# Zero columns in a turned weight, paired slope stores, and one norm asked for earlier, in a four-layer forward and backward pass

## Chip, cores and metric

The kernel runs on one core of one Trainium2 chip. The metric is device time in microseconds of one execution. Each kernel is executed several times, and the median of the runs is compared. One execution is also recorded by the hardware profiler; the views that are quoted come from that record.

## The reference

The reference is four residual layers and the gradients of all their inputs. Layers 0 and 2 are linear attention (A), layers 1 and 3 a gated block (B). S = 2048, D = 512, F = 1376, 32 heads of 16, everything in bfloat16. A and B use the same weights both times.

```
x = x + A(layernorm(x))        # wqkv, wo: phi(q) (phi(k)^T v), normalised, @ wo
x = x + B(layernorm(x))        # h = sigmoid(x @ w_gate) * (x @ w_up);  h @ w_down
x = x + A(layernorm(x))
x = x + B(layernorm(x))
out, vjp = jax.vjp(f, A_x, A_wqkv, A_wo, B_w_gate, B_w_up, B_w_down)
return out, *vjp(grad_out)
```

## The kernel before

The 2048 rows are 16 tiles of 128 rows (`st`), in 4 blocks of 4 tiles (`NBLK`, `NB`; a block has `SB` = 512 rows). The F = 1376 columns are 11 chunks of 128 (`NFC`). 1376 is 10 x 128 + 96, so the last chunk overlaps the one before it: `FC0[10]` is 1248, and its first 32 columns (`FDUP`) are columns that chunk 9 holds too. Work on chunk 10 must not count these 32 twice.

The order of the work is written out by hand with Python generators: while layer l goes through its blocks, steps of the next layer are put between its chunks. Each engine runs its own list in order, and a tile framework adds the semaphores. TensorE (PE) has the matmuls, VectorE (DVE), ScalarE (ACT) and GpSimd (POOL) the elementwise work; SyncE (SP) issues most DMAs in one order, POOL some stores.

**Forward of layer 1** is `b_fwd`. For each block and chunk `glu` (L641 to L663) makes g and u (8 matmuls of 128 x 512), then on ACT the tanh (L655) and the slope's first half into `sd` (L656), on DVE `hh` (L657), and the second half of `sd` either on DVE (L659, `fused`, every odd chunk) or on ACT and POOL (L661, L662). `sd` tiles hold two chunks each and come from a pool of 7 slots, which attention's `pe_t` tiles share in part of the time. `store` (L677 to L679) writes `hh` and `sd` to DRAM when the next chunk is under way, on SP. At the start of the next block `down` (L682 to L690) multiplies `hh` with w_down: for each of 4 tiles chunks 0 to 9, and then chunk 10 for the 4 tiles.

**The norm ahead of a layer** is `LN.one`. For layer 1 it goes in pairs of tiles: the squares on ACT (L315), the reciprocal root on POOL (L317, L318), the norm on DVE (L320), the transposed copy `hT` by a DMA transpose on SP (L323). `AFwd.out` asks for the norm of a pair as soon as layer 0's output of that pair is added; a condition on L583 leaves out the last pair of a block in blocks 1, 2 and 3 of layer 0. Those pairs (tiles 6 and 7, 10 and 11, 14 and 15) are then asked for at chunk 10 of the block of layer 1 that goes before (`ln.need` in `b_fwd`).

**Layer 3** is `b_both`, forward and backward in one. It needs w_down turned (`wdT`, three DMA transposes by `turn_wd`, which cut w_down as `SETS` does: 512, 512 and 352 columns) and w_up and w_gate turned (`wuT`, `wgT`). The latter are loaded by `load_b_bwd` while block 0 goes through its chunks: for each one DMA transpose of chunks 0 to 9, one of chunk 10, and then a POOL memset that clears the first 32 rows of chunk 10. Per chunk `b_both` makes g, u and the gradient `dhh` (4 matmuls on `wdT`), on DVE `scale` multiplies `dhh` into `sd`, which is from then on the gradient `dd`. In blocks 1 to 3 `turn_dd` turns each chunk by a DMA transpose into `nat_t` tiles of 4 chunks, which `flush_nat` stores; block 0 stores its chunks unturned. At chunk 2 of block 1 (chunk 1 later) come `down` of the block before (4 x 11 matmuls, L728) and `dh_b` (L819 to L826), which goes through the 11 chunks of `wuT` and then the 11 of `wgT` for each tile.

**Later**, `wdT` comes back from DRAM (`wdT_d`) for layer 1's backward, `b_bwd`, which also loads the stored slopes (`sh_t`, 4 or 3 chunks a load). Everything after that is the weights' gradients.

Of the kernel before, what the change touches and what calls it, by code (L numbers as in the profile page):

```python
# [69 lines left out]
@with_exitstack  # L70
def kernel(
    ctx: ExitStack,
    tc: tile.TileContext,
    A_x: bass.AP,
    A_wqkv: bass.AP,
    A_wo: bass.AP,
    B_x: bass.AP,
    B_w_gate: bass.AP,
    B_w_up: bass.AP,
    B_w_down: bass.AP,  # L80
    grad_out: bass.AP,
    out_0: bass.AP,
    out_1: bass.AP,
    out_2: bass.AP,
    out_3: bass.AP,
    out_4: bass.AP,
    out_5: bass.AP,
    out_6: bass.AP,
):
    nc = tc.nc  # L90
    assert tuple(A_x.shape) == (1, S, D) and tuple(grad_out.shape) == (1, S, D)
    assert tuple(A_wqkv.shape) == (D, 3 * D) and tuple(A_wo.shape) == (D, D)
    assert tuple(B_w_gate.shape) == (D, F) and tuple(B_w_up.shape) == (D, F) and tuple(B_w_down.shape) == (F, D)
    k = K()
    k.nc, k.tc = nc, tc
    k.st = nc.gpsimd
    k.x_in = A_x.rearrange("b s d -> (b s) d")
    k.g_in = grad_out.rearrange("b s d -> (b s) d")
    k.out0 = out_0.rearrange("b s d -> (b s) d")
    k.out1 = out_1.rearrange("b s d -> (b s) d")  # L100
    k.outs = dict(wqkv=out_2, wo=out_3, wg=out_4, wu=out_5, wd=out_6)
    k.w_in = dict(wqkv=A_wqkv, wo=A_wo, wg=B_w_gate, wu=B_w_up, wd=B_w_down)

    pool = lambda name, bufs, **kw: ctx.enter_context(tc.tile_pool(name=name, bufs=bufs, **kw))
    consts, resid, k.keep = pool("consts", 1), pool("resid", 1), pool("keep", 1)

    k.small = pool("small", 6)
    k.p_h, k.p_hT = pool("h", 4), pool("hT", 4)
    dram = pool("dram", 1, space=DRAM)

    build_consts(k, consts)
    k.xs = [resid.tile([P, D], F32, name=f"x{st}") for st in range(NST)]
    k.sv = []
    for l in range(4):
        d = dict(h=dram.tile([S, D], BF16, name=f"sv_h{l}"))
        if l % 2 == 0:
            for nm in ("dqT", "dkT"):
                d[nm] = dram.tile([D, S], BF16, name=f"sv_{nm}{l}")
            for nm in ("hT", "pkT", "qr", "qn"):
                d[nm] = dram.tile([NBLK, P, (2 if nm == "qr" else 1) * NB * D], BF16, name=f"sv_{nm}{l}")  # L120
            d["E"] = dram.tile([D, D], BF16, name=f"sv_E{l}")
            d["M"] = dram.tile([D, D], BF16, name=f"sv_M{l}")
            d["kvT"] = dram.tile([NDC * P, P], BF16, name=f"sv_kvT{l}")
            d["CT"] = dram.tile([D, D], BF16, name=f"sv_CT{l}")
            d["dkvT"] = dram.tile([NDC * P, P], BF16, name=f"sv_dkvT{l}")
        else:
            d["hhT"] = dram.tile([F, S], BF16, name=f"sv_hhT{l}")
            d["ddT"] = dram.tile([2, F, S], BF16, name=f"sv_ddT{l}")
            if l == 3:
                d["g"] = k.g_in  # L130
                d["wd"] = dram.tile([F, D], F32, name="sv_wd3")
                d["ddN"] = dram.tile([NBLK, len(SETS), P, 2, NB, D], BF16, name="sv_ddN3")
            else:
                d["g"] = dram.tile([S, D], BF16, name=f"sv_g{l}")
                d["sd"] = dram.tile([NBLK, NFC, P, 2 * SB], BF16, name=f"sv_sd{l}")
        k.sv.append(d)
    k.rstd = [k.keep.tile([P, NST], F32, name=f"rstd{l}") for l in range(4)]
    k.A = {l: {} for l in (0, 2)}
    k.wT = [dram.tile([P, NDC * D], BF16, name=f"wT{i}") for i in range(6)]
    k.wdT_d = dram.tile([P, NDC * F], BF16, name="wdT_d")  # L140
    k.turned = []
    k.gns, k.gTs, k.nats = {}, {}, []

    k.wb = ExitStack()
    k.ps = pool("ps", 4, space=PSUM)
    forward(k)
    backward(k)


# [275 lines left out]

def turn_wd(k, t, i):
    c0, w = SETS[i]
    k.nc.sync.dma_start_transpose(out=t[:, :, c0:c0 + w], in_=k.w_in["wd"][c0:c0 + w, :])


def load_b_bwd(k, t, nm, first):
    nc = k.nc
    held(k, first, nc.sync.dma_start_transpose(out=t[:, 0:NFC - 1, :], in_=k.w_in[nm][:, 0:(NFC - 1) * P]))
    nc.sync.dma_start_transpose(out=t[:, NFC - 1, :], in_=k.w_in[nm][:, F - P:F])
    nc.gpsimd.memset(t[0:FDUP, NFC - 1, :], 0.0)


def add_x(k, st, y_ps, x=None):
# [8 lines left out]
class AFwd:  # L447
# [130 lines left out]
    def out(self, b, j):  # L578
        k, nxt = self.k, self.nxt
        y_ps = k.bank([P, D], F32, name="y_ps")  # L580
        mm4(k, y_ps[:], lambda c: self.pe[b, c // 2][:, 0, c % 2, rows(j)], lambda c: self.M[:, c, :])
        add_x(k, b * NB + j, y_ps, None if self.l else narrow(k, b * NB + j))
        if j % 2 and (b < 2 or self.l == 0) and not (b and j == NB - 1 and self.l == 0):  # L583
            nxt.need(b * NB + j)

    def second(self, nxt):
# [32 lines left out]
        for nm, t in (("E", E), ("M", M), ("kvT", kvT)):  # L619
            k.st.dma_start(out=sv[nm][:].rearrange("(c p) e -> p c e", p=P), in_=t[:])  # L620
        if l == 2:
            k.wdT = k.p_wa.tile([P, NDC, F], BF16, name="wdT", tag="wkvo")
            turn_wd(k, k.wdT, 0)
            last_grads(k, 0)
        for j in range(NB):
# [45 lines left out]
def b_fwd(k, l, ln, nxt):  # L671
    nc, sv = k.nc, k.sv[l]
    hhs, late = {}, []

    def store():

        b, fc, hh, sd = late.pop()  # L677
        store_hh(k, sv, b, fc, hh, nc.sync)
        nc.sync.dma_start(out=sv["sd"][b, fc], in_=sd.rearrange("p a b -> p (a b)"))  # L679

    def down(b):
        ys = [k.bank([P, D], F32, name="y_ps") for _ in range(NB)]  # L682
        for fcs in (range(NFC - 1), (NFC - 1,)):
            for j in range(NB):
                for fc in fcs:
                    nc.tensor.matmul(ys[j][:], lhsT=hhs[b][fc][:, rows(j)], rhs=k.wd[:, fc, :],
                                     start=(fc == 0), stop=(fc == NFC - 1))
        for j in range(NB):
            add_x(k, b * NB + j, ys[j])

    for b in range(NBLK):
        hhs[b] = []
        if b:
            down(b - 1)
        for fc in range(NFC):
            hh, sd = glu(k, ln.hT[b], fc, fc % 2 == 1, b == fc == 0)
            hhs[b].append(hh)
            if late:
                store()
            late.append((b, fc, hh, sd))  # L700
            if fc == NFC - 1:
                ln.need((b + 1) * NB + NB - 1)
            if b and fc in (2, 4):
                nxt.need((b - 1) * NB + (1 if fc == 2 else 3))
            yield b, fc
    store()
    down(NBLK - 1)
    nxt.need(NST - 1)
# [10 lines left out]
def b_both(k, l, ln, ctx):  # L719
# [17 lines left out]
    def scale(b, fc, dhh, dd):  # L737
        k.last_mul = nc.vector.tensor_tensor(dd, dhh[:].unsqueeze(1).to_broadcast([P, 2, SB]), dd, ALU.mult)  # L738
        if b:
            turn_dd(k, sv, b, fc, dd)  # L740
        else:
            store_dd(k, sv, b, fc, dd, nc.sync)

    late = []
    for b in range(NBLK):
# [4 lines left out]
        for fc in range(NFC):  # L750
            hh, dd = glu(k, ln.hT[b], fc, first=b == fc == 0)
            ps = k.bank([P, SB], F32, name="dhh_ps")
            mm4(k, ps[:], lambda c: k.wdT[:, c, FC0[fc]:FC0[fc] + P], lambda c: gTs[b][:, c, :])
            dhh = k.p_dhh.tile([P, SB], BF16, name="dhh_t")
            nc.scalar.mul(dhh[:], ps[:], 0.5)
            if late:
# [35 lines left out]
def turn_dd(k, sv, b, fc, dd):  # L792

    i, f = divmod(fc, 4)
    p0 = FDUP if fc == NFC - 1 else 0
    if f == 0:
        k.nat = k.p_nat.tile([P, 2, NB, D], BF16, name="nat_t")
    k.nc.sync.dma_start_transpose(
        out=k.nat[:, :, :, f * P - p0:(f + 1) * P - p0].rearrange("p a j f -> p (a j) f"),
        in_=dd.rearrange("p a s -> p (a s)"))  # L800
    if f == 1:
        flush_nat(k)
    if f == 3 or fc == NFC - 1:
        w = SETS[i][1]
        k.nats.append((sv["ddN"][b, i, :, :, :, 0:w], k.nat[:, :, :, 0:w]))

# [26 lines left out]
def backward(k):  # L833
    nc, tc = k.nc, k.tc
    with ExitStack() as ctx:
# [8 lines left out]
        k.woT = wab.tile([P, NDC, D], BF16, name="woT")  # L844
        k.wqkvT = wab.tile([P, 3 * NDC, D], BF16, name="wqkvT")
        sv, k.n_t, k.turn = k.sv, NB, True
        k.wdT = w_pool(k, "wdT").tile([P, NDC, F], BF16, name="wdT")
        k.fill = Fill(k)
        a_bwd(k, 2, False)
        b_bwd(k, 1)  # L850
# [48 lines left out]
def b_bwd(k, l):  # L899
    nc, sv = k.nc, k.sv[l]  # L900
    with ExitStack() as ctx:
# [23 lines left out]
        for b in range(NBLK):  # L925
            for f0, nf in FGRP:
                sh = k.p_sh.tile([P, 4, 2, SB], BF16, name="sh_t", tag="sh")
                nc.sync.dma_start(out=sh[:, 0:nf].rearrange("p f a s -> p f (a s)"),
                                  in_=sv["sd"][b, f0:f0 + nf].rearrange("f p s -> p f s"))
                for fc in range(f0, f0 + nf):  # L930
                    i = fc - f0
                    ps = k.bank([P, SB], F32, name="dhh_ps")
                    mm4(k, ps[:], lambda c: k.wdT[:, c, FC0[fc]:FC0[fc] + P], lambda c: gTs[b][:, :, c, :])
                    dhh = p_g.tile([P, SB], BF16, name="dhh_t")
                    nc.scalar.mul(dhh[:], ps[:], 0.5)  # L935
                    dd = p_dd.tile([P, 2, SB], BF16, name="dd_t")
# [363 lines left out]
```

## Time and profile before

| quantity | value |
|---|---|
| runs (us) | 1104.85, 1107.46, 1107.54, 1108.09, 1112.91 |
| median of the runs | 1107.54 |
| profiled execution, its own time | 1108.09 |
| its span, first to last instruction | 1106.1 |
| mean granted TensorE clock | 0.997 |
| PE, share of the span | 96% |
| DVE, ACT, POOL | 50%, 40%, 27% |
| mean DMA rate | 235 GB/s |

The span is what the record covers; the own time also has what lies around it (1.99 us). In lines of a timeline the first number is the start in us from the span's start, the second the time from the first to the last instruction of the group, then engine, line, operation, result and inputs, sizes, the number of instructions, and in brackets how long the engine stood idle before it and what released it. In the view of waits the three numbers are the total, the number of times and the longest. In the view of stretches the first numbers are the stretch and its length, then the busy time of PE, weight loads, DVE, ACT and POOL, and at the end the granted clock, the share of the DMA engines in use (it can pass 1) and GB/s.

### The profile page before, as it was taken

How to read it: one execution, taken by the hardware profiler on the slowest of the kernel's cores; microseconds unless marked ns; L12 is line 12 of the kernel's file. 1: busy time of each engine (PE TensorE's matmuls, PEld its weight loads, DVE VectorE, ACT ScalarE, POOL GpSimd, SP SyncE). 2: the span in 40 equal slices, each digit the busy share in tenths (PEclk: the TensorE clock that was granted, in tenths of full speed). 3: DMA queues.
4: the chain of work that ended last, by engine and by line, in shares of the span. 5: the costliest groups of instructions: out<-in, count | busy, mean ns of one | idle time of the engine just before them, and what ended most of it. 6: DMA issues, size and time to landing. Idle time of an engine off the chain costs nothing.

```text
span 1106.1 us, 15309 instructions
## 1 busy us (share of the span) xinstructions
PE 1065.0 (96%) x5448; PEld 494.7 (45%) x5448; DVE 552.9 (50%) x1029; ACT 445.4 (40%) x930; POOL 302.9 (27%) x404
## 2 busy tenths in 40 slices
PE   6989899999999999999999999999999999999998
PEld 3444343444434444444444444444444444465443
DVE  7686764669825445444767435556876200001110
ACT  4476775547744646453224434434235200000010
POOL 5333433203632616141532210002623100011120
PEclk9999999999999999999999999999999999999999
DMA  9987987689995979799997997868989899599990
GB/s 268 277 234 241 282 219 221 197 199 230 299 226 120 272 181 266 210 231 281 318 326 213 225 269 221 241 183 243 357 250 337 221 244 216 124 204 255 268 207 31
DMA packets 394972, 259.99 MB, mean 235 GB/s; under 512 B 305744, under 2 KB 356720, under 8 KB 393872
## 3 DMA queue, kind: packets, MB, share of 16 engines
q1 hardware_dynamic: 379648, 208.91, 75.4%
q0 software_dynamic: 15248, 50.11, 13.2%
q8 instruction: 42, 0.69, 0.3%
q14 instruction: 34, 0.28, 0.1%
HBM read 77.73 MB, written 106.76 MB: 167 GB/s over the span
## 4 chain that ended last, share of the span: by engine, by line
PE 53%; DMA 3%; issue 2%; ACT 2%; POOL 1%; DVE 1%; SPq 0%; ACTq 0%; DVEq 0%; POOLq 0%
PE dw_ps L1244 18%; PE dh_ps L916 7%; PE dhh_ps L196 4%; PE dh_ps L1089 4%; PE dh_ps L825 3%; PE dw_ps L1262 3%; PE dpk_ps L196 2%; PE dh_ps L1080 2%; PE CT_ps L1009 2%; PE y_ps L196 2%; PE fill_ps L252 1%; PE dq_ps L196 1%; PE g_ps L196 1%; PE u_ps L196 1%; DMA qp_l<-sv_qr 1%
## 5 line engine op out<-in xcount | busy, mean ns | idle before, releaser
L1244 PE MATMUL dw_ps<-set_t,rows_t 128*128 128x512 bf16 (+1 forms) x1024 | 204.4, 362 | 0.0
L1244 PEld LDWEIGHTS <-rows_t 128*128 128x128 bf16 x1024 | 100.1, 98 | 103.6
L662 POOL TENSOR_TENSOR sd_t<-sd_t,hh_t 128x512 bf16<-128x512 bf16 x68 | 81.4, 1197 | 156.2 <-DVE hh_t L657 104.6
L1169 DVE CAST dw_new<-dw_ps 128x512 bf16<-128x512 f32 (+1 forms) x20 | 12.4, 653 | 186.9 <-PE dw_ps L1244 160.9
L1169 ACT CAST dw_new<-dw_ps 128x512 bf16<-128x512 f32 (+1 forms) x20 | 10.5, 561 | 225.7 <-PE dw_ps L1244 188.1
L886 ACT ACTIVATE t_sb<-dh_ps,rstd 128x512 f32<-128x512 f32 x64 | 43.5, 680 | 129.3 <-PE dh_ps L825 90.0
L196 PE MATMUL g_ps<-hT_t,wg 128*128 128x512 bf16 (+1 forms) x360 | 91.6, 377 | 3.8 <-DMA hT_t<-h_t 2.5
L196 PE MATMUL dhh_ps<-gT_t,wdT 128*128 128x512 bf16 x352 | 90.5, 379 | 2.9 <-ACT dhh_t L935 2.9
L196 PE MATMUL u_ps<-hT_t,wu 128*128 128x512 bf16 (+1 forms) x360 | 91.6, 377 | 0.5 <-DVE hh_t L657 0.2
L916 PE MATMUL dh_ps<-wgT,dd_t 128*128 128x512 bf16 x176 | 66.7, 379 | 0.0
L916 PE MATMUL dh_ps<-wuT,dd_t 128*128 128x512 bf16 x176 | 66.7, 379 | 0.0
L657 DVE SCALAR_TENSOR_TENSOR hh_t<-sd_t,u_ps 128x512 bf16<-128x512 bf16 x88 | 59.5, 679 | 10.2 <-ACT sd_t L656 9.5
L738 DVE TENSOR_TENSOR sd_t<-dhh_t,sd_t 128x1024 bf16<-128x1024 bf16 x44 | 30.4, 690 | 63.0 <-POOL sd_t L662 61.6
L1170 POOL DMA_DIRECT2D out_dram<-dw_new x36 | 19.3, 541 | 155.5 <-DVE dw_new L1169 136.0
L656 ACT ACTIVATE sd_t<-g_ps,onef 128x512 bf16<-128x512 f32 x88 | 60.4, 690 | 2.6
L937 DVE TENSOR_TENSOR dd_t<-dhh_t,sh_t 128x1024 bf16<-128x1024 bf16 x44 | 29.9, 690 | 60.5 <-ACT dhh_t L935 55.0
L655 ACT ACTIVATE g_ps<-g_ps 128x512 f32<-128x512 f32 x88 | 52.5, 600 | 11.7 <-PE g_ps L196 11.3
L196 PEld LDWEIGHTS <-wg 128*128 128x128 bf16 x360 | 34.6, 98 | 45.4 <-issue 3.8
L196 PEld LDWEIGHTS <-wdT 128*128 128x128 bf16 x352 | 34.4, 98 | 44.6 <-issue 3.7
L196 PEld LDWEIGHTS <-wu 128*128 128x128 bf16 x360 | 35.4, 98 | 42.1 <-issue 1.8
L825 PEld LDWEIGHTS <-sd_t 128*128 128x128 bf16 x352 | 34.5, 98 | 41.5
L916 PEld LDWEIGHTS <-dd_t 128*128 128x128 bf16 x352 | 34.4, 98 | 41.6
(167 smaller groups left out, 1837.2 us busy)
## 6 DMA issues: line engine op xcount, KB each, us to landing
sv_sd<-sd_t SPq DMA_DIRECT2D x44, 256.0 KB, 3.3
sv_ddT<-dd_t SPq DMA_DIRECT2D x40, 256.0 KB, 4.8
sv_h<-h_t POOLq DMA_DIRECT2D x16, 512.0 KB, 5.1
sv_qr<-pe_t POOLq DMA_DIRECT2D x16, 512.0 KB, 5.1
sh_t<-sv_sd SPq DMA_DIRECT2D x8, 1024.0 KB, 6.6
rows_t<-sv_h SPq DMA_DIRECT2D x16, 512.0 KB, 6.8
sv_ddN<-nat_t SPq DMA_DIRECT2D x6, 1024.0 KB, 4.8
set_t<-sv_ddN SPq DMA_DIRECT2D x12, 512.0 KB, 6.6
```

The costliest lines, as they stand in the source:

```text
L196: i = k.nc.tensor.matmul(out, lhsT=lhs(c), rhs=rhs(c), start=(c == 0), stop=(c == n - 1))
L655: nc.scalar.activation(g_ps[:], g_ps[:], ACT.Tanh, scale=-0.5)
L656: nc.scalar.activation(sd[:, 0, :], g_ps[:], ACT.Identity, bias=k.onef[:], scale=-1.0)
L657: nc.vector.scalar_tensor_tensor(hh[:], sd[:, 0, :], 0.5, u_ps[:], ALU.mult, ALU.mult)
L662: nc.gpsimd.tensor_tensor(sd[:, 1, :], sd[:, 1, :], hh[:], ALU.mult)
L738: k.last_mul = nc.vector.tensor_tensor(dd, dhh[:].unsqueeze(1).to_broadcast([P, 2, SB]), dd, ALU.mult)
L825: k.nc.tensor.matmul(dh_ps[:], lhsT=dds[fc][:, a, rows(j)], rhs=(k.wuT, k.wgT)[a][:, fc, :], start=(i == 0), stop=(i == 2 * NFC - 1))
L886: nc.scalar.activation(t_sb[:], dh_ps, ACT.Identity, scale=rstd, accum_out=c1[:])
L916: nc.tensor.matmul(acc[b][j][:], lhsT=dd[:, a, rows(j)], rhs=(k.wuT, k.wgT)[a][:, fc, :], start=(fc == 0 and a == 0), stop=(fc == NFC - 1 ...
L1089: nc.tensor.matmul(dh[j][:], lhsT=lhs(j, c), rhs=rhs(c), start=False, stop=stop and c == NDC - 1)
L1244: k.nc.tensor.matmul(ps[ic][:, 0:w], lhsT=h_m[:, ic * P:(ic + 1) * P], rhs=t_m, start=(m == 0), stop=(m == n - 1))
L1262: k.nc.tensor.matmul(p[0:r, :], lhsT=t[:, f:f + r], rhs=g_t, start=(i == 0 and st == 0), stop=(i == len(srcs) - 1 and st == NST - 1))
```

## The change

Four edits, the first and the last of which belong together:

1. `wdT` gets 11 x 128 = 1408 columns instead of 1376. Chunk 10 is columns 1280 to 1407 of it, of which the first 32 are cleared by one POOL memset and the other 96 are w_down's last rows, turned by a DMA transpose of their own. `dhh` of chunk 10 is then zero in its first 32 rows, and `wuT` and `wgT` are no longer cleared there. `wdT_d` in DRAM grows with it.
2. The slopes of layer 1 are stored two chunks at a time, in a DRAM layout that has the partition first.
3. The condition on L583 now leaves out the last pair only where b is 1. The norms of tiles 10, 11 and of 14, 15 are asked for as soon as layer 0's output is added.
4. `turn_dd` turns chunk 9 after chunk 10: chunk 10's turned form has 32 columns of zeros that lie where chunk 9's last 32 columns go, and chunk 9 overwrites them.

```diff
-                d["sd"] = dram.tile([NBLK, NFC, P, 2 * SB], BF16, name=f"sv_sd{l}")
+                d["sd"] = dram.tile([P, NBLK * NFC, 2 * SB], BF16, name=f"sv_sd{l}")
...
-    k.wdT_d = dram.tile([P, NDC * F], BF16, name="wdT_d")
+    k.wdT_d = dram.tile([P, NDC * NFC * P], BF16, name="wdT_d")
...
 def turn_wd(k, t, i):
     c0, w = SETS[i]
+    n = (NFC - 1) * P
+    if i == len(SETS) - 1:
+        k.nc.gpsimd.memset(t[:, :, n:n + FDUP], 0.0)
+        k.nc.sync.dma_start_transpose(out=t[:, :, n + FDUP:], in_=k.w_in["wd"][n:F, :])
+        w = n - c0
     k.nc.sync.dma_start_transpose(out=t[:, :, c0:c0 + w], in_=k.w_in["wd"][c0:c0 + w, :])
...
     nc.sync.dma_start_transpose(out=t[:, NFC - 1, :], in_=k.w_in[nm][:, F - P:F])
-    nc.gpsimd.memset(t[0:FDUP, NFC - 1, :], 0.0)
...
-        if j % 2 and (b < 2 or self.l == 0) and not (b and j == NB - 1 and self.l == 0):
+        if j % 2 and (b < 2 or self.l == 0) and not (b == 1 and j == NB - 1 and self.l == 0):
             nxt.need(b * NB + j)
...
-        nc.sync.dma_start(out=sv["sd"][b, fc], in_=sd.rearrange("p a b -> p (a b)"))
+        n = b * NFC + fc
+        if n % 2:
+            nc.sync.dma_start(out=sv["sd"][:, n - 1:n + 1], in_=sd[:].rearrange("p n a s -> p n (a s)"))
...
         if b:
+            if fc == NFC - 2:
+                return
             turn_dd(k, sv, b, fc, dd)
+            if fc == NFC - 1:
+                turn_dd(k, sv, b, fc - 1, dds[b][fc - 1])
...
-            mm4(k, ps[:], lambda c: k.wdT[:, c, FC0[fc]:FC0[fc] + P], lambda c: gTs[b][:, c, :])
+            mm4(k, ps[:], lambda c: k.wdT[:, c, rows(fc)], lambda c: gTs[b][:, c, :])
...
-    if f == 3 or fc == NFC - 1:
+    if f == 3 or fc == NFC - 2:
...
-                                  in_=sv["sd"][b, f0:f0 + nf].rearrange("f p s -> p f s"))
+                                  in_=sv["sd"][:, b * NFC + f0:b * NFC + f0 + nf])
```

`dhh` in layer 1's backward uses `rows(fc)` of `wdT` in the same way.

More of the change, by code (lines that the diff above doesn't have):

```diff
@@ L621, in second @@
         if l == 2:
-            k.wdT = k.p_wa.tile([P, NDC, F], BF16, name="wdT", tag="wkvo")
+            k.wdT = k.p_wa.tile([P, NDC, NFC * P], BF16, name="wdT", tag="wkvo")
             turn_wd(k, k.wdT, 0)
@@ L699, in b_fwd @@
                 store()
-            late.append((b, fc, hh, sd))
+            late.append((b, fc, hh, k.sd2))
             if fc == NFC - 1:
@@ L846, in backward @@
         sv, k.n_t, k.turn = k.sv, NB, True
-        k.wdT = w_pool(k, "wdT").tile([P, NDC, F], BF16, name="wdT")
+        k.wdT = w_pool(k, "wdT").tile([P, NDC, NFC * P], BF16, name="wdT")
         k.fill = Fill(k)
@@ L932, in b_bwd @@
                     ps = k.bank([P, SB], F32, name="dhh_ps")
-                    mm4(k, ps[:], lambda c: k.wdT[:, c, FC0[fc]:FC0[fc] + P], lambda c: gTs[b][:, :, c, :])
+                    mm4(k, ps[:], lambda c: k.wdT[:, c, rows(fc)], lambda c: gTs[b][:, :, c, :])
                     dhh = p_g.tile([P, SB], BF16, name="dhh_t")
```

## The prediction

> **What bounds the kernel now.** I read the page's engine table first, then the waits of PE, then the timeline around its long waits, and last the granted clock in those stretches.
>
> ```profile
> PE 1065.0 (96%) x5448; PEld 494.7 (45%) x5448; DVE 552.9 (50%) x1029; ACT 445.4 (40%) x930; POOL 302.9 (27%) x404
> ```
>
> PE is busy for 1065.0 of 1106.1 us, so it is idle for 41.1 us. The change leaves the number and the order of PE's instructions alone. The time can therefore move only through PE's waits and through its clock. The next view lists what PE waited for, by total:
>
> ```profile
> PE y_ps L196 <- DVE hh_t L657: 2.7, 1, 2.7
> PE g_ps L196 <- DMA hT_t<-h_t: 2.5, 1, 2.5
> ...
> PE y_ps L686 <- DVE hh_t L657: 2.0, 1, 2.0
> ```
>
> These three single waits lie at edited code; the rest of the 41 us does not. PE's timeline places two of them:
>
> ```profile
> 167.22 9.66 PE L686 MATMUL y_ps<-wd,hh_t 128*128 128x512 bf16 x44
> 179.41 1.74 PE L196 MATMUL g_ps<-hT_t,wg 128*128 128x512 bf16 x4 [2.53 <-DMA hT_t<-h_t]
> ...
> 316.60 7.29 PE L196 MATMUL y_ps<-wd,hh_t 128*128 128x512 bf16 x33
> 326.58 4.10 PE L196 MATMUL y_ps<-wd,hh_t 128*128 128x512 bf16 x11 [2.70 <-DVE hh_t L657]
> 330.52 2.54 PE L825 MATMUL dh_ps<-wuT,sd_t 128*128 128x512 bf16 x11
> ```
>
> The first is block 3 of layer 1, waiting for the transposed norm of tiles 14 and 15. The second is the last output tile of block 0 in layer 3. It is put down to DVE, whose hh frees a PSUM bank, but DVE itself had stood 12.29 us behind a POOL product, and POOL's timeline shows why:
>
> ```profile
> 323.58 0.51 POOL L435 MEMSET wuT<- 32x512 bf16 x1 [11.03 <-DMA wuT<-in_B_w_up_dram]
> 324.06 1.14 POOL L662 TENSOR_TENSOR sd_t<-sd_t,hh_t 128x512 bf16<-128x512 bf16 x1
> ```
>
> A memset of 0.51 us waits for the load of wuT, and product, DVE and PE wait behind it. The last view gives stretches of PE, DVE, ACT and POOL with the granted clock third from the end:
>
> ```profile
> 179.60:183.00 3.40, 3.40 (x9) 1.18 (x8) 0.00 (x0) 1.82 (x5) 0.00 (x0) 0.50 0.00 1
> 326.30:329.80 3.50, 3.22 (x8) 1.13 (x8) 1.51 (x3) 0.32 (x1) 1.67 (x2) 0.51 1.08 245
> 135.20:138.60 3.40, 3.39 (x16) 1.57 (x17) 1.60 (x3) 0.08 (x1) 1.99 (x2) 1.00 1.01 353
> ```
>
> After each of the two long waits PE ran 3.4 us at half clock (8 or 9 matmuls instead of 16). After the 2.00 us wait at 135 it did not.
>
> **The sum is made against 1108.09 us**, the profiled execution (span 1106.1, and 1.99 around it), 0.55 above the median of the runs, 1107.54. A matmul of 512 columns takes 0.216 us (four in 0.86).
>
> **Norm no longer deferred (tiles 10, 11 and 14, 15 of layer 1).** Before, the norm of tiles 14 and 15 is asked for at chunk 10 of block 2: squares on ACT at 166.42 and 168.20, transpose issued on SP at 173.21, landed 6.2 later, 179.4. The rows of x were ready on DVE at 160.7. Now it is asked for right after them. Moved are one ln_neg, two squares (0.71 each), two POOL steps (0.19 and 0.71), two DVE norms (0.54) and the transpose on SP. On SP it now passes some seven stores (hhT and sd). I put its issue at 167 and its landing at 173 to 174, before 176.7, where PE asks. The wait of 2.53 goes, and with it the half clock behind it, 3.40 x 0.50 = 1.7. What is late next: the squares now stand ahead of chunk 9's tanh and slope on ACT. Its hh was done at 168.5 and is needed at 167.22 + 9 x 0.216 = 169.2. With two squares ahead I put it at 169.5, a new wait of 0.4 in the middle of down's matmuls, with all of PE's list behind it. Its ends are 0, the row where it was not late, and 2.0, the row of block 1; the value is nearest to zero because ACT only reorders work that it did anyway. In block 1 (tiles 10, 11) the same move puts POOL's rstd ahead of a product. The hh that ends the 2.00 us wait then comes 0.45 earlier: -0.45, with ends -0.5 and +1.1 (another product of 1.14 ahead of it). Sum of the part: -2.53 - 1.7 + 0.4 - 0.45 = -4.28.
>
> **No memsets of wuT and wgT.** POOL's product then runs when its inputs are there, near 313. The 2.70 wait goes, and its half clock, 3.50 x 0.49 = 1.7. What is late next: down(0) begins at 316.60 and takes 44 x 0.216 = 9.5, to 326.1; the 11 matmuls on wuT take 2.4, to 328.5. wuT's tail landed before 323.6, so nothing waits there. The first matmul on wgT then wants the body of that load:
>
> ```profile
> 321.42 5.59 SPq L433 DMA_TRANSPOSE wgT<-in_B_w_gate_dram  x1
> ...
> DMA to landing us min/median/max: 3.8/6.3/8.7
> ```
>
> It lands at 321.42 + 8.7 = 330.1; before, PE came there at 332.89 and waited for nothing. New wait 330.1 - 328.5 = 1.65, with all of PE's list behind it. Its ends are 0 (the load lands earlier, with SP less full) and 4.4 (the whole gain lost, because the stores that POOL held back now share the DMA engines, at a share of 1.08 already). I take 1.65, since nothing that the load itself waits for is edited. Sum: -2.70 - 1.7 + 1.65 = -2.75.
>
> **The zero columns.** One POOL memset of 128 x 128 elements is added: between 0.2 (Z_t, 128x128) and 0.51 (32x512). It waits for the matmuls that read wo (its slot held wo before) and stands ahead of the store of M, which waits for what those matmuls make; POOL idled 2.20 us there: nothing, and 0.5 for that store without the cover. The third turn of w_down (SP, 3.20 us at 264.17) becomes two transposes. The second costs SP some 1.25 (the row of wuT's tail), SP idles 267.4 to 269.6, and the columns are first used near 305: nothing. wdT goes to DRAM and back 2.3% larger (10 us a way); the load at 578.94 has 37 us before its first use: nothing. Chunk 9 turned after chunk 10 adds no instruction. It delays one store of a set and changes places on SP with one load of g. The next hf_t load still lands near 507.9 and is used at 513.45: a cover of 5.5 us.
>
> **Slopes stored in pairs.** 22 stores of 512 KB instead of 44 of 256 KB.
>
> ```profile
> L679 SPq DMA_DIRECT2D sv_sd<-sd_t x44: 319/520/1405, 78.6 to 205.4; - x44
> sv_sd<-sd_t SPq DMA_DIRECT2D x44, 256.0 KB, 3.3
> sv_hT<-hT_t SPq DMA_DIRECT2D x8, 512.0 KB, 4.3
> ```
>
> SP saves 22 x 0.52 = 11.4 us of issue between 77 and 205, where only the late transpose above waits on it; that is in the first part already. The landing of one pair is about 1 us later (4.3 against 3.3). A pair is stored when the next chunk is under way, 5.6 us after its slot was taken, so the slot is free near 10 us. While four of the seven slots hold pe_t (75 to 125 us, 19 chunks of 2.6 us), three slots cycle in 3 x 2 x 2.6 = 15.6. The cover is some 5.7 us: nothing. The loads of slopes in layer 1's backward move the same bytes: nothing.
>
> **Total:** -4.28 - 2.75 = -7.03, so 1108.09 - 7.0 = 1101.1.
>
> [...] The two half-clock terms rest on the rows 0.50 and 0.51. [...]
>
> **Rivals.** First, the next transfer takes the place of the memset: wgT lands later still, as the freed stores share its engines. For it: the share of DMA stands above 1.0 there. Against it: the load's own issue is untouched. Then layer 3 gains nothing, 1108.1 - 4.3 = 1103.8. Second, the half-clock stretches come back behind other waits (1.65 is not far from 2.53): 1108.1 - 3.6 = 1104.5; against it stands the 2.00 us wait with full clock after it. Third, on the other side, the pair holds its slot too long. It decides from a landing of 15.6 - 5.6 = 10 us; the longest of the 44 stores was 5.9. At 11.5 us each of some ten pairs up to 125 us holds ACT's next slope, and PE, for 1.5: +15 - 7 = +8, 1116. Fourth, the change does not do what it says: hT still lands behind the stores on SP, and other loads take the rest, near 1107.5.
>
> **How the numbers follow.** My forecast gets 0.55, the rivals 0.19, 0.09, 0.09 and 0.08. By 0.5% (5.5 us, about what a measurement of this kernel can tell from no change) faster means below 1102.0. The forecast's own range is 1099 (both new waits at zero) to 1103 (they double); about 0.44 of its 0.55 lies below 1102. The first rival gives 0.05 there, the second 0.01: faster 0.50. Slower, above 1113.1, is the third rival, 0.09. The rest, 0.11 + 0.14 + 0.08 + 0.08, is 0.41. The range runs from 1098.0 (the forecast's lower end, and a run 1 us below it; the five runs spread further) to 1107.5, the fourth rival's value, and leaves out the third.
>
> **What would show it.** Right: no PE wait for hT_t in layer 1; no memset at wuT or wgT; granted clock 1.00 in the stretches that answer to those at 0.50 and 0.51; a wait of about 1.6 us for wgT ahead of dh_ps; waits for hh at L686's matmuls of about 0.4 and 1.6; PE busy near 1061.6. Wrong: a wait for hT_t left, a wgT wait over 3 us, half clock behind it, or ACT waiting for sd stores.

## The result: no change that can be measured

The kernel before has a median of 1108.23 us (48 runs), the kernel after 1107.86 us (27 runs). The ratio of the times is 0.9994, with an interval of 0.9978 to 1.001. The forecast was 1101.1; the seven microseconds did not come. The ratios here and below are worked out from all runs of a round except a few slow ones, so they are not exactly the ratio of the two medians. Each round of experiments measured the kernel before anew (1107.52, 1109.08 and 1108.17).

The profiled execution of the kernel after took 1111.41 us (span 1109.7, granted clock 0.994), 3.6 above its median. Its PE waits at the places of the change, as the view of waits has them (total, times, longest, in us):

```profile
PE dh_ps L835 <- DMA wgT<-in_B_w_gate_dram: 4.3, 1, 4.3
...
PE y_ps L692 <- DVE hh_t L661: 3.0, 2, 2.2
```

The two waits that the change was expected to remove are gone: none for `hT_t` and none behind a memset. A wait of 4.3 us for the load of wgT has come, and the wait for `hh` in `down` has grown from one of 2.0 to two, together 3.0. PE's timeline puts them in place:

```profile
135.70 9.41 PE L692 MATMUL y_ps<-wd,hh_t 128*128 128x512 bf16 x35 [2.17 <-DVE hh_t L661]
...
172.82 7.73 PE L692 MATMUL y_ps<-wd,hh_t 128*128 128x512 bf16 x35 [0.81 <-DVE hh_t L661]
180.38 1.03 PE L196 MATMUL g_ps<-hT_t,wg 128*128 128x512 bf16 x4
...
315.91 9.66 PE L196 MATMUL y_ps<-wd,hh_t 128*128 128x512 bf16 x44
325.41 2.54 PE L835 MATMUL dh_ps<-wuT,sd_t 128*128 128x512 bf16 x11
332.27 4.85 PE L835 MATMUL dh_ps<-wgT,sd_t 128*128 128x512 bf16 x11 [4.33 <-DMA wgT<-in_B_w_gate_dram]
```

At 180.38 block 3 begins with no wait; at 315.91 all 44 matmuls of `down` run through. Then 11 matmuls on wuT, and PE stands until 332.27. The 11 matmuls behind the wait take 4.85 instead of 2.54: half clock again (granted 0.51 from 330.7 to 334.1).

PE's instructions stand in the same order in both kernels, so the n-th matmul of one execution can be set against the n-th of the other. The distance between their starts (after less before) steps as follows:

| place | forecast | in the two traces |
|---|---|---|
| hh of block 1, tiles 10 and 11's norm | -0.45 | +0.2, and +1.7 half clock behind it |
| hh of block 2 | +0.4 | +1.2 |
| hT of tiles 14, 15 with its half clock | -4.2 | -4.4 |
| memset of wuT with its half clock | -4.4 | -4.4 |
| load of wgT | +1.65 | +7.1 (4.5 wait, 2.6 half clock) |

Both gains came, within 0.2 of the forecast. They were given back at two places: in `down` of layer 1, and at wgT. The rows sum to +1.4. The last matmul begins 3.8 later than before: of the other 2.4 us, 0.6 lie at the start of the kernel and ahead of block 2's `down`, and 1.8 behind 500 us, at other waits. This is one execution against one; what was given back differs between executions, as the experiments show.

Why PE stood so long begins in SP's timeline; below it are the landings of wgT's two transposes, from the view of the tile:

```profile
320.79 8.09 SPq L438 DMA_TRANSPOSE wgT<-in_B_w_gate_dram  x1
```

```profile
DMA to landing us min/median/max: 3.5/7.5/11.4
```

The body was issued 0.6 us earlier than before and landed 11.4 us after its issue, not 8.7. Its issuing instruction alone took 8.09 on SP instead of 5.59. POOL's timeline shows what ran beside the two loads, where before POOL stood from 312.5 to 323.58:

```profile
313.51 0.58 POOL L672 DMA_DIRECT2D sv_hhT<-hh_t  x1
...
316.13 0.58 POOL L672 DMA_DIRECT2D sv_hhT<-hh_t  x1
...
318.76 0.58 POOL L672 DMA_DIRECT2D sv_hhT<-hh_t  x1
321.85 0.73 POOL L741 DMA_DIRECT2D out_dram<-o_t  x1 [2.51 <-DVE o_t L739]
326.59 0.73 POOL L741 DMA_DIRECT2D out_dram<-o_t  x1 [4.01 <-DVE o_t L739]
```

The DMA queues of the stretch 316 to 330, first in the kernel before and then in the kernel after, each with packets, MB and share of the engines:

```profile
q1 hardware_dynamic: 10579, 2.68, 107.2%
q0 software_dynamic: 71, 0.23, 4.8%
```

```profile
q1 hardware_dynamic: 8322, 2.11, 104.1%
q0 software_dynamic: 224, 0.66, 18.3%
```

q0 carries POOL's stores (with five of them put on SP, below, it moved nothing there). Before, POOL stood behind the memset and q0 moved 0.23 MB there; without the memset it moved 0.66. SP's queue q1, which has the transposes, got 8322 packets through instead of 10579, at about the same share of time.

### The profile page after: what moved, and what is told of

The parts are those of the page before. It is cut to its first block, busy times and chain, and to the rows that moved or that the text cites. A ratio compares the mean times of both kernels' runs of the same rounds, so it can differ in the third digit from the quotient of the medians.

```text
span 1109.7 us, 15238 instructions
## 1 busy us (share of the span) xinstructions
PE 1069.1 (96%) x5448; PEld 496.0 (45%) x5448; DVE 554.2 (50%) x1029; ACT 444.9 (40%) x930; POOL 300.7 (27%) x403
## 4 chain that ended last, share of the span: by engine, by line
PE 56%; DMA 2%; ACT 2%; issue 1%; DVE 1%; POOL 1%; ACTq 0%; SPq 0%; POOLq 0%; DVEq 0%
PE dw_ps L1254 18%; PE dh_ps L926 7%; PE dh_ps L1099 5%; PE dhh_ps L196 4%; PE dh_ps L835 3%; PE dw_ps L1272 3%; PE dh_ps L1090 2%; PE CT_ps L1019 2%; PE dpk_ps L196 2%; PE fill_ps L252 2%; PE y_ps L196 2%; PE dq_ps L196 2%; DMA qn_l<-sv_qn 1%; PE g_ps L196 1%; PE u_ps L196 1%
```

## The experiments

The theory after the result: the norm edit and the missing memsets do what was forecast, but each gives its gain to a wait beside it, and half clock comes as well behind a wait that leaves PE little work in one window of 3.413 us (0.88 and 0.92 us before, 0.51 to 1.23 after; the last section has the windows). The rivals: that a gain is lost in any case to whatever comes later, and that the long load was one execution's chance.

**Each part by itself.** The norm edit alone, on the kernel before:

```diff
-        if j % 2 and (b < 2 or self.l == 0) and not (b and j == NB - 1 and self.l == 0):
+        if j % 2 and (b < 2 or self.l == 0) and not (b == 1 and j == NB - 1 and self.l == 0):
```

> The kernel before with the norm edit alone. Theory (each part does what its traces show, and half clock comes only when most of one 3.41 us window is idle): the hT wait of 2.53 and about half a half-clock stretch (0.9) go, about 1.0 of new waits for hh come, so -2.4 against before, about 1105.8; in the trace no PE wait for hT_t, the memset wait near 2.7 still there, wgT's body lands 8 to 9 us after its issue. Rival (the norm's gain is given back to later waits whatever happens in layer 3): 0 within 0.8.

Measured 1106.24 against 1107.52, ratio 0.9991 (0.9956 to 1.0027). In its trace the hT wait is gone, the waits for hh are 2.2 and 0.8, a memset wait of 2.3 is there, and wgT's body landed after 8.6. The interval allows both theories; the trace shows the waits that the first one names, the memset's at 2.3 instead of about 2.7.

The same line of the diff reversed, on the kernel after:

> The kernel after with the old condition on the norm: zero columns, pairs and turn order only. Theory (the memset's wait is replaced by a longer one for wgT, because the stores that POOL now issues earlier share the DMA engines with the load): wgT's body lands 11 to 12 us after its issue, PE waits 4 to 4.5 for it with half clock behind, the hT wait of about 2.5 is back; +2.9 against before, about 1111. Rival (the long landing was one execution's chance): landing near 8.7, wait near 1.7, and -1 to -2.7 against before.

Measured 1111.26 against 1107.52, ratio 1.0019 (0.9988 to 1.005). Landing 11.1, wait for wgT 4.3 with half clock behind it (matmuls on wgT of up to 634 ns, with a median of 379), hT wait 2.9, one hh wait of 2.0. So the second hh wait, and the step from 2.0 to 2.2 of the first, belong to the norm edit.

The zero columns, the memsets' removal and the turn order alone (the diff's edits 1 and 4):

> The kernel before with the zero columns and the turn order alone. Theory: as with the old norm condition put back, wgT's body lands 11 or more us after its issue, PE waits 4 or more for it with half clock behind, the time is +1.5 to +3.5 against before. Rival (pairs are needed for the slow landing): landing under 9.5, wait under 2.5, -1 to -3.

Measured 1110.46 against 1109.08, ratio 1.001 (0.9987 to 1.0033). Landing 10.2, wait 3.1 with half clock behind it (matmuls of up to 631 ns): the sizes are below the forecast, and the time's +1.4 in the medians is within the noise. The pairs alone (edit 2):

> The kernel before with the slopes stored in pairs, alone. Theory (SP's time is not on the path): PE's waits stay, 2.5 for hT_t and 2.7 behind the memset within 0.4, no wait of ACT for sv_sd; 0 within 1 against before. Rival (SP's shorter list brings the late transpose forward): hT wait under 1.5, -1 to -2.5. Slower rival (a slot of the pairs held too long): ACT's slope waits for stores, +2 or more.

Measured 1111.10 against 1109.08, ratio 1.0004 (0.9978 to 1.0029): nothing that can be seen. ACT never waited for a store of sd, and the hT wait stayed at 2.8, so SP's shorter list alone did not bring the transpose forward. Its profile had something that nobody expected: the wait behind the memset was 10.9, not 2.7.

```profile
PE y_ps L196 <- DVE hh_t L657: 10.9, 1, 10.9
```

In this execution SP issued wuT's load at 320.78, 5.4 us after `down` had begun, and not 3.3 before it. More on that below.

**The load of wgT.** To test whether POOL's stores slow it, five of them go on SP's list behind it, in the kernel after:

```diff
-            store_hh(k, sv, b, fc, hh, k.st)
+            store_hh(k, sv, b, fc, hh, nc.sync if b == 1 and fc < 3 else k.st)
...
-                k.st.dma_start(out=by_tile(k.out0, st - 1, 2), in_=ost[:])
+                (k.st if b else nc.sync).dma_start(out=by_tile(k.out0, st - 1, 2), in_=ost[:])
```

> The kernel after with five stores (hhT of chunks 0 to 2 of block 1 and the two of out0's block 0) put on SP's list, where they stand behind wgT's load. If the freed stores are what slows the load: wgT's body lands 8 to 9.5 us after its issue, the wait for it falls from 4.33 to 1 to 2, and the time by 3 to 4.5 against after, about 1104. If the load is slow by itself: landing 11 or more, wait 4 or more, time unchanged within 1.

The load did as the theory has it. Landings and the start of the first wgT matmuls:

```profile
DMA to landing us min/median/max: 3.1/5.5/8.0
```

```profile
328.93 2.53 PE L835 MATMUL dh_ps<-wgT,sd_t 128*128 128x512 bf16 x11 [0.99 <-DMA wgT<-in_B_w_gate_dram]
```

8.0 instead of 11.4, and 0.99 of waiting with full clock behind it. In the stretch 316 to 330 q0 moved nothing, and q1 got 11340 packets through. But the time was 1107.27, ratio 0.9996 to the kernel before (0.9962 to 1.003), not 1104; its twelve runs go from 1099.39 to 1112.36. So four more profiled executions were taken, two of this kernel and two of the kernel after, to see whether that profile is typical.

> The kernel after with the five stores on SP, another execution. If loads that start late by chance take the gain: wgT's wait 2.5 or more in one of the two looks, though its body still lands within 9.5 of its issue. If the first profile is typical: wait 0.5 to 1.5 in both.

> The five stores on SP, a third execution. Late loads by chance: wait for wgT 2.5 or more in this look or in the one before. First profile typical: 0.5 to 1.5 in both.

> The kernel after, another execution. The wait for wgT between 3 and 10, half clock behind it; the block-1 wait for hh 2.2 again, with half clock behind it only when it falls in one window of the clock.

> The kernel after, a third execution. The wait for wgT between 3 and 10 with half clock behind it, and the block-1 wait for hh near 2.2.

Two of the four are like the first profiles: 0.77 of waiting with the stores on SP, 4.1 without. In the other two the load of wuT was itself late, and PE waited for both weights. First the waits of the kernel after, then those with the stores on SP:

```profile
PE dh_ps L835 <- DMA wuT<-in_B_w_up_dram: 3.4, 1, 3.4
...
PE dh_ps L835 <- DMA wgT<-in_B_w_gate_dram: 2.7, 1, 2.7
```

```profile
PE dh_ps L835 <- DMA wuT<-in_B_w_up_dram: 4.1, 1, 4.1
...
PE dh_ps L835 <- DMA wgT<-in_B_w_gate_dram: 3.0, 1, 3.0
```

Over all 18 profiled executions of this study wuT's load was issued 2.5 to 4.1 us before `down` began in 14, and 2.0 to 5.4 after it in 4. In three of the late ones (the pairs alone, and these two) SP had stood ahead of a store of turned queries until 314.9 to 318.5, where it goes on at 304.0 to 310.6 in the other fifteen, and everything behind it in its list moved. The timeline of SP in the late execution of the kernel after:

```profile
302.98 9.21 SPq L570 DMA_TRANSPOSE qn_t<-pe_t  x2
314.86 0.34 SPq L221 DMA_DIRECT2D sv_qn<-qn_t  x1
...
318.23 5.81 SPq L438 DMA_TRANSPOSE wuT<-in_B_w_up_dram  x1
```

The 2.7 for wgT in the kernel after is below the 3 to 10 that were expected, since PE had waited for wuT first. Why those transposes of queries were slow was not tested. The wait behind the memset has no fixed size either: 2.7 in the kernel before, 10.9 with the pairs alone. That late loads took the gain of the five stores is the likelier reading, not a proof: one late execution in three was seen for that kernel.

The landings in all 18 executions tell two causes of a long wait apart. With the memset (four executions) wgT's body landed 8.4 to 9.1 us after its issue, and wuT's 8.1 to 9.3. Without it and with the five stores behind the loads (four) it was 7.9 to 8.6 and 7.3 to 8.9. Without either (ten) it was 8.9 to 13.7 and 9.9 to 12.9. So the two loads take longer where the stores run beside them: wuT's landings stand apart without exception, wgT's but for one of 8.9. A load that SP issues late is a second thing, which came in each of the three groups.

The other way is to leave the load as it is and to ask for wgT later. In `dh_b` block 0 does the wuT half of all four tiles first and keeps four banks open:

```diff
-    for j in range(NB):
-        st = b * NB + j
-        dh_ps = k.bank([P, D], F32, name="dh_ps")
-        for i in range(2 * NFC):
-            a, fc = divmod(i, NFC)
...
+    n, ps = (1 if b else NB), {}
+    for j0 in range(0, NB, n):
+        for a in range(2):
+            for j in range(j0, j0 + n):
...
```

> The kernel after, with the gradient matmuls of block 0 in another order: the wuT half of all four tiles first, then the wgT half. First wgT matmul 7.1 us later. If the wgT wait is what took the memset's gain: no wait for wgT, no half clock near 330, -5.5 to -6.5 against after, about 1102. If the time is lost anyhow to what comes next (norm gradients now close together, banks): under -2.

Measured 1101.51 against 1107.52, ratio 0.9947 (0.9914 to 0.998). No wait is left there, and no half clock:

```profile
315.48 9.66 PE L196 MATMUL y_ps<-wd,hh_t 128*128 128x512 bf16 x44
325.06 9.66 PE L838 MATMUL dh_ps<-wuT,sd_t 128*128 128x512 bf16 x44
334.56 9.66 PE L838 MATMUL dh_ps<-wgT,sd_t 128*128 128x512 bf16 x44
```

The load was no faster (its body landed 9.3 after the issue, wuT's 12.0). What falls away is the place where PE needs it early. It is the most direct evidence that the wgT wait had swallowed the memset's gain. What this order does on the kernel before, where PE did not wait for wgT, was not measured.

**The waits for hh.** `down` of layer 1 in the kernel after, with the last two chunks instead of one held back to the second pass:

```diff
-        for fcs in (range(NFC - 1), (NFC - 1,)):
+        for fcs in (range(NFC - 2), (NFC - 2, NFC - 1)):
```

> The kernel after, with the forward's down in layer 1 split at chunk 9 and not at chunk 10: chunks 0 to 8 for the four tiles, then 9 and 10. If the waits of 2.2 and 0.8 for hh (and the half clock after the first) are what took back the norm's gain: both gone, no half clock near 136, -4 to -4.7 against after, about 1103.5; wgT's wait of 4.3 remains. If the time goes to what follows (the four tiles end close together, so the next block's g waits for banks or adds): under -1.5.

Measured 1104.34 against 1109.08, ratio 0.9947 (0.9923 to 0.9971). Block 2's wait is gone. Block 1's fell to 1.15, and 0.80 for an hT came behind it, so the part is not all gone, but the half clock went (wgT's wait was still 3.4 in its trace):

```profile
132.60 7.94 PE L692 MATMUL y_ps<-wd,hh_t 128*128 128x512 bf16 x36 [1.15 <-DVE hh_t L661]
141.34 1.02 PE L196 MATMUL g_ps<-hT_t,wg 128*128 128x512 bf16 x4 [0.80 <-DMA hT_t<-h_t]
```

**Both, and the edits again on that ground.** The two reorderings together, and once more with three variants beside it:

> The kernel after with down split at chunk 9 and with block 0's wuT half first. If both waits are independent, the gains add: -6 and -4.3, about 1097.5, granted clock near 0.998. If they are not, 1100 to 1102.

> The kernel with both reorderings (down split at chunk 9, wuT half first) once more, as the ground on which the next three stand. Within 2 of 1098.6.

Measured 1098.59 (ratio 0.9904, 0.9871 to 0.9937) and 1096.61 (0.9898, 0.9864 to 0.9932): about 11 us below the kernel before, and the fastest of the study. The gains add. How much of the 11 us the two reorderings would bring without the change is not shown: `down`'s wait of 2.0 stood in the kernel before too, and no run has them there alone. The next kernels say something of it. With the norm edit and both reorderings on the kernel before, so that the memsets are there and the pairs are not:

> The same two reorderings and the norm edit on the kernel before, without the zero columns and without the pairs: the memsets of wuT and wgT are back. Theory (taking the memsets away is worth its wait once nothing takes the wait's place): a wait of 2.3 or more behind the memset of wuT, some half clock, +3 to +6 against the kernel with both, about 1102.5. Rival (the zero columns are worth nothing even then): within 1.5 of it.

Measured 1103.39, ratio 0.9962 (0.9934 to 0.999), 4.8 and 6.8 above the two rounds of the kernel with both; the intervals overlap by a hair with the first and stand just apart from the second, which was measured in the same round. The wait behind the memset is back:

```profile
323.32 2.01 PE L196 MATMUL y_ps<-wd,hh_t 128*128 128x512 bf16 x5 [3.03 <-DVE hh_t L657]
```

So taking the memsets away is worth several microseconds where wgT is not the next to be late (the pairs, which this kernel lacks too, had shown no effect by themselves). It also leaves 4.8 us that the norm edit and the reorderings bring with the memsets in place. With the old condition on the norm:

> Both reorderings with the old condition on the norm. Theory (the norm edit is worth its 2.5 and part of a half-clock stretch once its successor waits are gone): the hT wait of 2.5 to 3 is back, +2.5 to +4 against the kernel with both, about 1102. Rival: within 1.5 of it, because hh waits elsewhere go with the old order.

Measured 1099.19, ratio 0.9928 (0.9901 to 0.9954), 0.6 and 2.6 above in the medians, with intervals that overlap. The expected hT wait of 2.5 to 3 did not come back at block 3: SP issued the late transpose 4.3 us after `down` had begun, against 5.9 with the old condition and the old `down`, and it landed in time. At block 2 PE waited 0.9 for hT, against 0.8 and 0.3 with both. What the norm edit is worth there stays open, and the theory is not confirmed. Last, the five stores on SP as well:

> Both reorderings and the five stores on SP's list behind wgT's load. Theory (with the wuT half first the load has 7 us more, so the stores' share of the DMA engines no longer matters): wgT's body lands 8 to 9.5 after its issue, not 13.7, no wait for it, and the time stays within 1.5 of the kernel with both. Rival (late loads still cost in some executions): -1.5 or more.

Measured 1097.74, ratio 0.9917 (0.9891 to 0.9943): no gain over the two reorderings, as expected. wgT landed 7.9 after its issue, and though wuT was issued 2.0 after `down` began, the view of waits has none for either.

## Why the prediction was wrong, by its steps

**The hT wait** was right in mechanism and size: -2.53 and its half clock, together -4.4 in the traces.

**hh behind the squares** was mis-sized. The prediction took 0.4 in block 2 from the end "nearest to zero"; it was 0.81, and 1.2 with what went before it: that ACT "only reorders work" did not keep the squares from making `hh` late. In block 1 it counted -0.45 because POOL's rstd comes first; the wait grew from 2.0 to 2.17 instead. That small step mattered: of the eight profiled executions with a wait of 2.17 to 2.19 there, six had half clock behind it (0.50 in the kernel after), and of the four with 2.0 none (1.00 before). Together the two terms were forecast at -0.05 and came to +3.1, half clock included.

**The memset's wait** was right as a term (-4.4). What took its place was named (the load of wgT) and wrongly priced: 1.65 against 4.33, and 2.6 of half clock. The failed step, and the larger of the two, is the sentence that nothing the load itself waits for is edited, which was the reason for the price. It waits for nothing new, but it shares the DMA engines with stores that the memset had held back, and so took 11.4 instead of 8.7. The first rival names this very mechanism, and the upper end of 4.4 that the prediction gave the wait was right; half clock behind the new wait was not in it. The forecast took the landing from a trace in which the competing stores stood still. The first rival's 1108.1 - 4.3 = 1103.8 was too low as well, because it left the hh terms as forecast and let the new wait cost no more than the old one.

**The pairs**: nothing that can be measured, as forecast. **The zero columns' own cost and the turn order** were forecast at nothing; PE's steps show nothing for them up to 500 us, and no run has them without the missing memsets. The slower rival (slots of the pairs) did not show: no wait of ACT for a store of sd.

**One execution as ground.** The prediction treated half clock as a fixed price of a long wait, and the memset's wait as a fixed 2.7. Both vary from one profiled execution to another: the wait was 2.7 in the kernel before, 2.3 with the norm edit alone and 10.9 with the pairs alone, and two executions of the kernel after had 0.50 behind a wait of 2.17 and 1.00 behind one of 2.19. In the rounds of experiments the runs of the kernel before with a granted clock of 0.997 or above have a median of 1106.0 (20 runs), those below 0.994 one of 1113.4 (16 runs). Time and clock go together there; how much of the 7.4 us is the half clock itself and how much the waits that bring it, the unprofiled runs don't show.

## What to carry to other kernels

When a wait is removed, look at what stood still during it: here the stores behind it ran beside the next load (0.66 MB instead of 0.23), and that load landed after 11.4 us, not after the 8.7 of the trace in which they waited. Where a late load is the successor, giving it other work to hide behind (here 7 us of matmuls that need only the first weight) brought 6 us, where making it faster brought nothing that could be measured. A likely reason is that it also covers executions in which the load starts late: in the one such execution with this order PE did not wait. A gain of a few microseconds that sits in single waits needs more than one profiled execution on each side.

## What the runs showed of the hardware

In the traces of the kernels before and after, half clock comes in stretches of 3.413 us with a granted clock of 0.50; one, in the kernel after, is 6.83 long. Within an execution their starts lie multiples of 3.413 apart: 179.60 and 326.37 before are 43 of them apart, 136.18, 330.74 and 559.43 after are 57 and 67. Cut into windows of 3.413 us that fit these starts, the window ahead of each stretch has PE busy for 0.88 and 0.92 us before, and for 1.23, 0.61 and 0.51 after. Of the other windows at full clock the least busy has 1.42 before (from 131.81) and 2.06 after (from 764.24), with 1.00 behind it. These are the windows from the first entry of the clock in the record to the last but one with matmuls. In the last one PE's list ends: it has 1.41 before, with 1.00 behind it, and 0.84 after, with 0.50. Block 1's wait shows both cases, first the kernel after with 2.17, then another execution of it with 2.19 (window and the one behind it, clock third from the end):

```profile
132.80:136.20 3.40, 1.23 (x7) 0.39 (x6) 2.97 (x5) 2.64 (x5) 2.35 (x3) 1.00 0.99 347
136.20:139.60 3.40, 3.40 (x10) 1.21 (x9) 0.64 (x2) 0.00 (x0) 1.14 (x1) 0.50 1.01 284
```

```profile
131.50:134.90 3.40, 1.52 (x7) 0.49 (x5) 2.16 (x3) 3.40 (x8) 2.04 (x4) 1.00 1.15 281
134.90:138.30 3.40, 3.09 (x15) 1.44 (x16) 1.45 (x3) 0.05 (x1) 1.94 (x2) 1.00 1.12 297
```

1.23 busy, then 0.50; 1.52 busy, then 1.00. The 2.00 us wait before was not followed by half clock, though it fell into one window whole: it left 1.42 us of work there, and the granted clock behind it was 1.00. So where PE had work to go on with, half clock stood behind full-clock windows with 1.23 us of work or less and not behind those with 1.42 or more. Where between the two it turns, and what turns it, these traces do not show.
